# Chunked attention with a spectral mixing layer on one core: the whole hand-written order of steps exchanged for another

## The chip, the core and the metric

One core of one Trainium2 chip runs the kernel. The metric is device time in microseconds (us) of one execution. Five engines work in parallel, each through its own instructions strictly in the order written: TensorE (PE, with its weight loads PEld), VectorE (DVE), ScalarE (ACT), GpSimd (POOL, which here issues all loads) and SyncE (SP, which issues most of the stores). Semaphores hold an instruction back until what it reads is written and what it overwrites has been read.

## What is computed

```python
q_c, k_c, v_c = (t.reshape(B, H, nc, 64, D) for t in (q, k, v))   # B=8, H=8, S=576=9*64, D=64
scores = scale * q_c @ k_c.transpose(...)           # 64 x 64 in each chunk
attn = softmax(scores)
x = (attn @ v_c)  -> [B, S, 512]
theta = x @ w_theta
zr, zi = x * cos(theta), x * sin(theta)
y = w_tok_r @ zr + w_tok_i @ zi                     # mixes the 576 tokens of a batch entry
u = x + y
out = u + max(u @ w_ch, 0)
```

Inputs are fp32 in DRAM; the loads turn them into fp16.

## The kernel before

The eight batch entries are worked in four pairs, 0 to 3. The 1,152 tokens of a pair are cut into five groups: A and B (256 tokens each of the pair's first entry), C and D (256 each of its second), and M, the 64 tokens left over from each entry together (128). All work is cut into small steps, and the string `ORDER` at the top of the file lists them, 584 in all. A loop at the end runs over that string and emits the instructions of each step; the order of the string is therefore the order of each engine's instructions, and the scheduler changes nothing in it. A step reads `kind.pair-group.bank`: `F.1C.2.4` is step F for group C of pair 1 in PSUM banks 2 and 4. A digit behind the kind (`V0`, `H1`) is half of the group's step: half of the heads, or one of two token tiles. There are eight PSUM banks of 128x512 fp32, shared by name: a step that writes a bank waits until the last reader of that bank is done.

The steps, in the order in which a group goes through them:

| step | engine | what it does, and where |
|---|---|---|
| qF, kF, q, k | POOL | loads of q and k of a group (`load_qk`); one DMA each, 256 KB as written; for M two each |
| v | POOL | load of v of a group (`load_v`), three DMAs of 128, 64 and 64 KB; for M two |
| lt, lc, lw | POOL | loads of w_theta, w_ch, and the two token matrices |
| F, FL, N, L, T | PE | transposes of q and k (`qk_t`): F is 64 transposes of 64x64, line 301; FL 32 of 128x64, line 316; for M, N 8 of 128x128 (line 335), L 16 of 128x64, T 32 of 64x64 (line 352) |
| tq, tqA, tk.. | DVE, ACT | their copies out of PSUM; A or V names the engine (`qk_copy`) |
| S, e | PE, ACT | scores (line 405); exp (line 422) |
| V, n | PE, DVE | attention times v (line 440); division by the row sums (lines 452 and 454) |
| X, Q and xA, xV | PE, then ACT or DVE | transpose of x, 8 of 128x128 (X, line 478) or 32 of 64x64 (Q, line 487), and its copy |
| H, g, z | PE, ACT, DVE | x times w_theta (line 518); cos and sin (lines 532, 536); the products zr and zi |
| TW, twA, twV, jw | PE, ACT, DVE | transposes of the token matrices, their copies and sums |
| YA to YM, y | PE, DVE | token mixing of pair 0, one group of inputs at a time; addition to x |
| ja to jd, Ka to Km, ra to rh | DVE, PE, DVE | token mixing of the other pairs by seven block products over sums of z (Ka .. Km: line 693), and their additions |
| U, R and uA, uV | PE, then ACT or DVE | as X and Q, of u |
| W, w, s, sA | PE, DVE, SP or ACT | u times w_ch (line 518), relu and addition, store |
| D | PE | dummy matmuls on zeros; their results are not used |
| pe, pg | ACT | a tiny exp or sin, ahead of the real ones, so that ACT loads the table of that function early; without one the first real exp or sin after the other function loads it |

Loads of pairs 1 to 3 are held back: ahead of each stands a tiny POOL copy (`gate`, line 170) that reads the result of the last n step emitted so far. All loads go through one queue on POOL and land mostly in the order in which they were issued.

The core of the loop:

```python
    with tc.manual_schedule():
        for step in ORDER:
            kind, at, *bank = step.split(".")
```

Of the kernel before, what the change touches and what calls it, by code (L numbers as in the profile page):

```python
# [23 lines left out]
V1.0B.6 kF.1D kF.1A qF.2A xV0.0A kF.2A v.1C V1.0M.1 n1.0B H0.0A.0 g0.0A qF.1B kF.1B H1.0A.3 q.1M
k.1M n1.0M v.1D X0.0B.1 n0.0M TW.03.4 X.0M.2 lc.00 xV0.0B H0.0B.1 z.0C X1.0B.0 TW.02.6 v.1A
xV.0M H.0M.2 twA.03 TW.01.4 z0.0A twA.02 z.0D g.0M xV1.0B TW.00.6 twV.01 twV.00 jw.00 g0.0B
H1.0B.0 qF.2B g1.0B z.0M F.1C.2.4 tqA.1C tkA.1C YC.0C.6 z1.0B YD.0C.6 z0.0B YM.0C.6 S.1C.4 g1.0A
FL.1A.0 FL.1D.2 e.1C y.0C FL.2A.6 YB.0A.4 tkA.1D tqA.1D z1.0A v.2A tq.1A tkA.1A YM.0A.4 S.1D.2
e.1D YA.0A.4 y.0A YB.0B.0 V0.1C.2 qF.2D tqA.2A tkA.2A F.1B.4.5 n0.1C tq.1B V1.1D.6 YA.0B.0
U.0A.2 n1.1D tkA.1B V0.1D.6 S.1B.4 e.1B uV.0A YM.0B.0 W.0A.2 n0.1D V1.1C.4 y.0B S.1A.6 e.1A  # L30
lw.04 X.1D.0 N.1M.1 xA.1D tkA.1M v.1M n1.1C YM.0D.4 w.0A kF.2D YD.0D.4 V0.1A.2 S.2A.6 tq.1M
S.1M.0 e.1M n0.1A v.2C jw.01 YC.0D.4 y.0D e.2A Q.1C.0 xA.1C V1.1A.6 n1.1A H.1D.2 V1.2A.0 V0.2A.4
H.1C.6 n1.2A V1.1M.0 n0.2A pg.00 g.1D V0.1M.1 Q.1A.4 qF.2C U.0D.2 n0.1M X.2A.3 v.1B xV.1A uV.0D
g.1C TW.04.1 n1.1M xA.2A H.1A.4 twA.04 X.1M.0 H.2A.6 kF.2B Y.0M.1 F.2D.2.3 v.3D z.1D v.2M g.1A
g.2A V1.1B.4 tqA.2D z.1C jc.1D z.1A Ka.1A.6 xA.1M y.0M n1.1B ja.1C v.2D tkA.2D F.2B.0.1 qF.3D
V0.1B.4 H.1M.2 tqA.2B n0.1B q.2M g.1M ra.1A q.3M U.0B.3 uA.0B X.1B.0 xV.1B W.0D.4 jb.1D H.1B.2
kF.3D z.1M Kf.1C.6 k.2M tkA.2B Ke.1C.0 g.1B kF.2C w.0D rc.1C S.2D.2 pe.00 e.2D z.1B R.0C.4 v.2B
Kg.1D.6 uV.0C re.1D W.0C.2 N.2M.4 rg.1B w.0C tkV.2M Km.1D.6 rf.1D tqA.2M Kc.1D.0 sA.0A S.2B.2
e.2B V1.2D.6 rd.1C FL.2C.4 qF.3A V0.2D.0 tkA.2C n1.2D n0.2D Kb.1B.2 qF.3B X.2D.0 U.0M.1 v.3B
z.2A rb.1A uV.0M W.0B.6 kF.3A s.0D tqA.2C qF.3C S.2C.4 S.2M.2 s.0C w.0B s.0B xA.2D W.0M.0 w.0M  # L40
e.2C V0.2B.6 n0.2B V1.2C.4 n1.2C v.3C U.1D.1 e.2M uV.1D H.2D.2 V0.2M.0 V1.2M.4 V0.2C.6 n0.2C
n0.2M v.3M Y.1M.5 pg.00 g.2D Q.2C.6 xA.2C V1.2B.0 jd.1B kF.3B W.1D.2 n1.2B y.1M H.2C.0 g.2C z.2D
w.1D s.1D X.2B.5 xA.2B n1.2M Kd.1B.6 z.2C R.1A.0 s.0M F.3A.2.3 uA.1A tqA.3A rh.1B H.2B.4 tkA.3A
X.2M.0 ja.2C jb.2D Ka.2A.6 W.1A.2 xA.2M g.2B ra.2A H.2M.0 F.3D.1.4 w.1A R.1C.2 g.2M uA.1C jc.2D
tqA.3D k.3M z.2M Kf.2C.6 Ke.2C.2 W.1C.0 tkA.3D rc.2C Kg.2D.6 re.2D w.1C S.3D.0 S.3A.4 Kc.2D.2
pe.00 e.3D z.2B e.3A rg.2B rd.2C kF.3C Km.2D.6 v.3A V1.3A.0 n1.3A F.3C.5.4 tqA.3C rf.2D Y.2M.3
tkA.3C S.3C.0 V0.3A.4 FL.3B.6 y.2M e.3C tqA.3B n0.3A V0.3C.0 T.3M.2 tkA.3B n0.3C tkV.3M U.1M.4
tqA.3M uV.1M X.3A.5 Kb.2B.0 xV.3A jd.2B R.1B.2 uV.1B s.1A rb.2A V1.3C.6 n1.3C H.3A.4 pg.00 g.3A
V0.3D.2 W.1B.0 R.2C.6 Q.3C.4 uA.2C n0.3D Kd.2B.2 w.1B S.3M.0 xV.3C pe.00 e.3M s.1B S.3B.4 e.3B
rh.2B H.3C.6 V1.3D.0 z.3A pg.00 g.3C n1.3D V1.3B.2 W.2C.4 n1.3B s.1C w.2C X.3D.0 W.1M.1 w.1M  # L50
R.2D.6 R.2B.4 V1.3M.3 xA.3D n1.3M uA.2D V0.3M.2 H.3D.0 uA.2B n0.3M z.3C g.3D Q.3M.6 V0.3B.4
xA.3M W.2D.2 n0.3B ja.3C Q.3B.4 xA.3B z.3D w.2D R.2A.0 jb.3D Ka.3A.6 uA.2A H.3M.5 jc.3D g.3M
W.2A.0 s.2C H.3B.2 g.3B w.2A ra.3A z.3M Ke.3C.4 re.3D W.2B.0 Kf.3C.6 w.2B s.2B sA.1M rc.3C
Kc.3D.4 z.3B Kg.3D.6 jd.3B sA.2D Kb.3B.0 rg.3B Km.3D.6 rd.3C Y.3M.2 rb.3A R.3A.0 y.3M sA.2A
rf.3D Kd.3B.4 uA.3A R.3D.6 R.3C.0 uA.3C rh.3B uA.3D W.3A.2 w.3A sA.3A W.3C.0 w.3C R.3B.6 uV.3B
s.3C R.3M.2 uA.3M W.3D.4 w.3D sA.3D W.3B.0 w.3B s.3B U.2M.7 uA.2M W.3M.2 w.3M s.3M W.2M.7 w.2M
sA.2M
""".split()


# [794 lines left out]
```

## Time and profile before

| | us |
|---|---|
| median of 3 runs | 205.39 (205.13 to 206.38) |
| the profiled execution | 204.54 |
| its span (first to last recorded event) | 202.8 |
| busy: PE / DVE / ACT / POOL | 190.6 / 148.3 / 120.8 / 83.2 |
| dummy matmuls (line 280) among PE's | 11.8, 39 matmuls |
| ACT table loads | 10 of 1.28 each |

Busy times are sums over the span of one profiled execution; matmuls overlap in the pipeline, so that a matmul's own 0.38 us stands for 0.22 us of progress in a row of them. The execution profiled is 0.85 us below the median of the runs.

### The profile page before, as it was taken

Reading aid. Unit: us, or ns where it says so; the run is one execution under the profiler, and the core shown is the slowest. Engines: PE = TensorE matmul, PEld = TensorE weight load, DVE = VectorE, ACT = ScalarE, POOL = GpSimd, SP = SyncE. Lnnn points to the kernel's source line nnn. Section 1 sums busy time; section 2 is a strip of 40 time slices with the busy share of each in tenths; the row PEclk is TensorE's granted clock in tenths of the full one; section 3 lists DMA queues with packets and bytes.
Section 4 is the critical chain, followed back from the end, with each engine's and each line's share of the span. In section 5 each row is a group of like instructions: output and inputs, shape, how many; then the busy total and the mean of one; then the engine's idle time right before and its main releaser. Section 6 shows DMA issues by size and latency. Waiting matters only on the chain.

```text
span 202.8 us, 7586 instructions
## 1 busy us (share of the span) xinstructions
PE 190.6 (94%) x3409; PEld 102.4 (51%) x3409; DVE 148.3 (73%) x235; ACT 120.8 (60%) x147; POOL 83.2 (41%) x135
## 2 busy tenths in 40 slices
PE   7696889999999999999999999999999999999990
PEld 3353555657556465545655554546544554444540
DVE  0123557984386888898988996978787999896671
ACT  2181498898545898973458296935869884101410
POOL 7967958556965478993084480000000000000000
PEclk9997999999999999999999999999999999999999
DMA  5999999999999969999989999300005200720176
GB/s 63 194 167 169 143 177 202 196 188 171 141 169 149 85 68 134 98 149 210 273 92 184 171 195 105 108 3 3 3 3 210 103 3 5 257 105 0 43 270 207
DMA packets 70431, 26.44 MB, mean 130 GB/s; under 512 B 47232, under 2 KB 65792, under 8 KB 70400
## 3 DMA queue, kind: packets, MB, share of 16 engines
q0 software_dynamic: 65408, 16.54, 87.1%
q1 hardware_dynamic: 3312, 6.29, 8.8%
q10 hardware_dynamic: 1680, 3.15, 4.4%
q8 instruction: 26, 0.43, 0.9%
q14 instruction: 5, 0.04, 0.1%
HBM read 33.06 MB, written 9.44 MB: 210 GB/s over the span
## 4 chain that ended last, share of the span: by engine, by line
PE 86%; POOL 4%; DMA 4%; DVE 2%; issue 1%; ACT 1%; DVEq 0%; POOLq 0%
PE ps L518 32%; PE ps L693 21%; PE ps L604 8%; PE ps L590 4%; DMA v<-in_v_dram 4%; PE ps L478 4%; PE ps L440 3%; PE ps L487 3%; PE ps L316 3%; PE ps L405 3%; POOL qk L181 2%; POOL v L232 2%; PE ps L301 2%; PE ps L269 2%; PE ps L280 1%
## 5 line engine op out<-in xcount | busy, mean ns | idle before, releaser
L232 POOL DMA_DIRECT2D v<-in_v_dram x48 | 36.1, 770 | 3.4 <-issue 1.5
L518 PE MATMUL ps<-wtheta,xT 128*128 128x512 f16 x144 | 34.7, 380 | 0.0
L518 PE MATMUL ps<-wch,uT 128*128 128x512 f16 x144 | 34.0, 380 | 0.0
L712 DVE TENSOR_TENSOR x<-ps,x 128x1024 f16<-128x1024 f32 x24 | 29.1, 1220 | 5.2 <-PE ps L693 4.9
L532 ACT ACTIVATE cos<-ps,pihalf 128x1024 f16<-128x1024 f32 (+1 forms) x22 | 21.1, 959 | 13.9 <-PE ps L518 11.5
L733 DVE SCALAR_TENSOR_TENSOR o<-ps,x 128x1024 f32<-128x1024 f32 (+1 forms) x20 | 22.2, 1116 | 6.5 <-PE ps L518 6.1
L454 DVE TENSOR_TENSOR x<-ps,recip 128x512 f16<-128x512 f32 (+1 forms) x40 | 25.5, 638 | 1.4
L422 ACT ACTIVATE eT<-ps 128x1024 f16<-128x1024 f32 (+1 forms) x18 | 16.5, 929 | 14.1 <-PE ps L405 14.0
L501 ACT COPY uT<-ps 128x1024 f16<-128x1024 f16 (+1 forms) x12 | 11.1, 943 | 20.0 <-PE ps L487 16.8
L372 ACT COPY kT<-ps 128x1024 f16<-128x1024 f16 (+1 forms) x18 | 16.6, 927 | 10.3 <-PE ps L301 5.4
L518 PEld LDWEIGHTS <-uT 128*128 128x128 f16 x144 | 13.2, 98 | 14.8 <-ACT uT L501 0.4
L518 PEld LDWEIGHTS <-xT 128*128 128x128 f16 x144 | 12.8, 98 | 13.9 <-issue 0.3
L370 ACT COPY qT<-ps 128x1024 f16<-128x1024 f16 (+2 forms) x15 | 12.9, 859 | 10.7 <-DVE kT L368 4.4
L536 ACT ACTIVATE sin<-ps 128x1024 f16<-128x1024 f32 (+1 forms) x22 | 19.0, 864 | 0.0
L693 PE MATMUL ps<-z,wT 128*128 128x512 f16 x72 | 18.8, 379 | 0.1
L452 DVE RECIPROCAL recip<-ps 128x8 f32<-128x8 f32 (+1 forms) x40 | 7.9, 196 | 14.3 <-PE ps L440 14.3
L604 PE MATMUL ps<-z,wT 128*128 128x512 f16 x72 | 16.7, 380 | 0.2 <-issue 0.2
L693 PE MATMUL ps<-zsum,wsum 128*128 128x512 f16 x72 | 16.7, 379 | 0.0
L693 PEld LDWEIGHTS <-wsum 128*128 128x128 f16 x96 | 9.1, 98 | 10.8
L280 PE MATMUL ps<-zeros 128*128 128x512 f16 x39 | 11.8, 457 | 2.9 <-issue 1.7
L693 PEld LDWEIGHTS <-wT 128*128 128x128 f16 x96 | 8.8, 98 | 9.8 <-issue 0.5
L723 DVE TENSOR_TENSOR x<-ps,x 128x1024 f16<-128x1024 f32 (+1 forms) x8 | 7.6, 954 | 7.7 <-PE ps L604 5.9
(68 smaller groups left out, 284.8 us busy)
## 6 DMA issues: line engine op xcount, KB each, us to landing
out_dram<-o SPq DMA_DIRECT2D x11, 512.0 KB, 3.5
qk<-in_q_dram POOLq DMA_DIRECT2D x16, 256.0 KB, 7.3
qk<-in_k_dram POOLq DMA_DIRECT2D x16, 256.0 KB, 6.9
v<-in_v_dram POOLq DMA_DIRECT2D x40, 64.0 KB, 5.1
out_dram<-o ACTq DMA_DIRECT2D x5, 512.0 KB, 3.2
v<-in_v_dram POOLq DMA_DIRECT2D x16, 128.0 KB, 6.1
wnat<-in_moe_w_tok_r_dram POOLq DMA_DIRECT2D x2, 288.0 KB, 7.5
wnat<-in_moe_w_tok_i_dram POOLq DMA_DIRECT2D x2, 288.0 KB, 7.9
```

Source lines behind the costliest of these rows:

```text
L232: nc.gpsimd.dma_start(v16[rows, slot + tile, :, 0:D], v[2 * p + bb, :, t0 : t0 + m, :].rearrange("h s d -> s h d"),)
L280: nc.tensor.matmul(psum(bank, 1), zeros[:, 0:P], zeros)
L372: nc.scalar.copy(out=t.rearrange("p x s c -> p x (s c)").rearrange("p x (c s) -> p x c s", s=n), in_=ps.rearrange("p x s c -> p x c s"),)
L422: nc.scalar.activation(out=eT.rearrange("p h r e c -> p (h r e) c"), in_=ps, func=AF.Exp, scale=scale)
L454: nc.vector.tensor_tensor(out=tokens(p, g, "x")[:, :, f * NE * D : (f + 1) * NE * D].rearrange("p c (h d) -> p c h d", h=NE), in0=psv[:, 0 ...
L518: nc.tensor.matmul(ps[:, a * DM : a * DM + cols.stop - cols.start], xT[:, b0 + a, db, :], weight[:, db, cols], start=(db == 0), stop=(db = ...
L532: nc.scalar.activation(out=cos[:, 0:n].rearrange("p a e -> p (a e)"), in_=pin, func=AF.Sin, bias=pihalf, scale=1.0,)
L536: nc.scalar.activation(out=sin[:, 0:n].rearrange("p a e -> p (a e)"), in_=pin, func=AF.Sin)
L604: nc.tensor.matmul(ps[:, a * DM : a * DM + DM], wT[:, kt, t0 : t0 + P], zs[bb], start=(done + k == 0), stop=(done + k == NK - 1),)
L693: nc.tensor.matmul(ps[:, a * DM : a * DM + DM], wt, zt, start=fresh and i == 0, stop=i == len(terms) - 1, skip_group_check=to in ("x", "z"),)
L712: nc.vector.tensor_tensor(out=u, in0=st[p]["ps_k", frm], in1=u, op=ALU.add)
L733: nc.vector.scalar_tensor_tensor(out=o, in0=ps[:, 0 : n * m].rearrange("p (j d) -> p j d", j=n), scalar=0.0, in1=u, op0=ALU.max, op1=ALU.add,)
```

## The change

Only the string `ORDER` is another; the functions that it calls are the same. It has 581 steps. Both orders begin with pair 0. Up to the first token mixing they read (before with -, after with +):

```diff
-qF.0C init.00 kF.0C D.12.0 id.00 D.6.0 F.0C.0.1 tkA.0C qF.0D kF.0D tq.0C S.0C.0 FL.0D.2 tkA.0D
-qF.0A kF.0A v.0C e.0C tq.0D D.8.6 S.0D.6 FL1.0A.0 FL0.0A.2 tq0.0A e.0D tqA1.0A v.0D D.6.4
-V0.0D.4 n0.0D qF.0B tkA0.0A S0.0A.2 tkA1.0A V1.0D.6 n1.0D e0.0A kF.0B D.7.0 FL0.0B.0 tqA0.0B
-tkA0.0B FL1.0B.6 V0.0C.4 q.0M n0.0C V1.0C.2 n1.0C k.0M N1.0M.0 N0.0M.1 tq0.0M tqA1.0M tkA1.0B
-S0.0B.4 X.0C.2 tq1.0B tkV0.0M e0.0B S1.0A.6 e1.0A v.0A lt.00 v.0B S1.0B.4 X.0D.3 xV.0C tkV1.0M
-S1.0M.6 V1.0A.0 xV.0D v.0M e1.0B e1.0M V0.0A.4 n1.0A S0.0M.2 e0.0M H.0C.6 n0.0A pg.00 g.0C
-X1.0A.0 lw.02 lw.00 X0.0A.1 qF.1C V0.0B.2 n0.0B kF.1C H.0D.4 xA1.0A V0.0M.2 g.0D qF.1A qF.1D
...
+qF.0A kF.0A id.00 init.00 D.12.0 qF.0D D.5.0 FL1.0A.0 kF.0D FL0.0A.2 tqA1.0A tq0.0A tkA1.0A
+S1.0A.0 tkA0.0A F.0D.7.6 tq.0D tkA.0D D.5.2 S.0D.2 e1.0A S0.0A.4 e0.0A v.0A qF.0C D.2.0 V0.0A.0
+qF.0B V1.0A.4 n0.0A kF.0B D.6.0 FL0.0B.0 e.0D FL1.0B.2 kF.0C F.0C.6.7 tkA0.0B tqA0.0B n1.0A
+X1.0A.4 tkA.0C tq1.0B v.0D X0.0A.5 D.3.0 V0.0D.0 tq.0C q.0M k.0M n0.0D lt.00 xV0.0A tkA1.0B
+S1.0B.2 V1.0D.6 n1.0D e1.0B S.0C.0 L0.0M.2 L1.0M.3 e.0C tkV0.0M tkV1.0M X.0D.5 xV.0D tq1.0M
+tqA0.0M S0.0B.0 e0.0B S0.0M.6 S1.0M.0 e1.0M H.0D.2 xV1.0A e0.0M v.0C V0.0C.0 V1.0C.4 pg.00 g.0D
+n0.0C n1.0C H1.0A.7 H0.0A.6 v.0B V1.0B.0 n1.0B v.0M lw.02 Q.0C.4 xA.0C g1.0A V0.0M.2 n0.0M g0.0A
+V0.0B.0 V1.0M.3 H.0C.4 lw.00 qF.1C kF.1C n0.0B X0.0B.0 n1.0M qF.1A kF.1A X1.0B.1 z.0D xV1.0B
+Q.0M.2 xA.0M qF.1B kF.1B v.1C TW.02.6 twV.02 H.0M.3 g.0C TW.03.1 twA.03 q.1M k.1M xV0.0B z1.0A
+z.0C H1.0B.0 v.1A g.0M z0.0A qF.2A v.1D TW.01.6 twV.01 H0.0B.1 g0.0B z.0M TW.00.4 F.1C.3.2 tq.1C
+twA.00 jw.00 YD.0D.6 g1.0B z1.0B YC.0D.6 F.1A.0.1 tkA.1C S.1C.2 pe.00 e.1C YM.0C.4 tq.1A YM.0D.6
...
+V0.1B.6 YM.0B.2 n0.1B z.1C YB.0B.2 e.1D y.0B FL.2A.0 qF.2B tqA.2A V1.1D.6 q.2M V0.1D.4 n0.1D
...
+z.1M v.3D e.2D tqA.2B kF.3D Kg.1D.2 rg.1B X.2A.0 xV.2A Ke.1C.4 re.1D tkA.2B v.2M Km.1D.2 qF.3B
...
```

The pair-0 loads before come as q and k of C, D and A, then v of C and D, q and k of B and M, v of A, w_theta, v of B and M, token matrices. After they come as q and k of A and D, v of A, q and k of C and B (q.C, q.B, k.B, k.C), v of D, q and k of M, w_theta, v of C, B and M, token matrices. The steps that are counted otherwise over the whole string:

| step | before | after |
|---|---|---|
| dummy matmuls in the D steps | 39 | 33 |
| full q, k transposes as FL / F, halves counted as halves | 8 / 8 | 3 / 13 |
| M's q, k transposes as N / L / T, two halves as one | 3 / 0 / 1 | 2 / 2 / 0 |
| X / Q of groups A to D, two halves as one; of M | 11 / 5; 3 / 1 | 10 / 6; 1 / 3 |
| U / R of groups A to D; of M | 4 / 12; 3 / 1 | 6 / 10; 2 / 2 |
| copies of q, k, x, u and the token matrices on ACT / DVE, steps | 61 / 32 | 58 / 35 |
| pg / pe steps | 5 / 3 | 7 / 3 |
| changes of ACT's table between exp and sin, by the order of e and g | 9 | 13 |

More of the change, by code (lines that the diff above doesn't have):

```diff
@@ L23 @@
-X1.0A.0 lw.02 lw.00 X0.0A.1 qF.1C V0.0B.2 n0.0B kF.1C H.0D.4 xA1.0A V0.0M.2 g.0D qF.1A qF.1D
[L24 to L57, printed above, removed]
+qF.0A kF.0A id.00 init.00 D.12.0 qF.0D D.5.0 FL1.0A.0 kF.0D FL0.0A.2 tqA1.0A tq0.0A tkA1.0A
+S1.0A.0 tkA0.0A F.0D.7.6 tq.0D tkA.0D D.5.2 S.0D.2 e1.0A S0.0A.4 e0.0A v.0A qF.0C D.2.0 V0.0A.0
@@ new lines @@
+Q.0M.2 xA.0M qF.1B kF.1B v.1C TW.02.6 twV.02 H.0M.3 g.0C TW.03.1 twA.03 q.1M k.1M xV0.0B z1.0A
+z.0C H1.0B.0 v.1A g.0M z0.0A qF.2A v.1D TW.01.6 twV.01 H0.0B.1 g0.0B z.0M TW.00.4 F.1C.3.2 tq.1C
+twA.00 jw.00 YD.0D.6 g1.0B z1.0B YC.0D.6 F.1A.0.1 tkA.1C S.1C.2 pe.00 e.1C YM.0C.4 tq.1A YM.0D.6
+y.0D YC.0C.4 tkA.1A z0.0B F.1B.0.1 qF.1D kF.1D V0.1C.2 v.1B S.1A.6 lw.04 tq.1B YD.0C.4 e.1A y.0C
+n0.1C kF.2A lc.00 tkA.1B YA.0A.6 V1.1A.0 n1.1A V0.1A.4 YB.0A.6 v.1M V1.1C.0 n0.1A S.1B.2 L.1M.4
+qF.2C e.1B X.1A.5 qF.2D xA.1A n1.1C X.1C.0 kF.2C YM.0A.6 U.0D.1 H.1A.2 xV.1C pg.00 g.1A tq.1M
@@ new lines @@
+uV.0D H.1C.0 tkV.1M kF.2D F.1D.5.4 tkA.1D y.0A jw.01 v.2A R.0C.6 g.1C tq.1D uV.0C YA.0B.2 S.1D.4
+V0.1B.6 YM.0B.2 n0.1B z.1C YB.0B.2 e.1D y.0B FL.2A.0 qF.2B tqA.2A V1.1D.6 q.2M V0.1D.4 n0.1D
+W.0D.2 S.1M.4 k.2M n1.1D w.0D X.1D.6 kF.2B TW.04.7 tkA.2A e.1M v.2D twV.04 V1.1M.0 V0.1M.1
+S.2A.2 xA.1D e.2A V1.1B.4 n1.1B n0.1M z.1A H.1D.6 n1.1M X.1B.5 pg.00 g.1D xV.1B W.0C.2 w.0C
+ja.1C R.0A.0 X.1M.4 uA.0A sA.0C z.1D qF.3A jc.1D U.0B.5 H.1B.6 uA.0B v.2C g.1B xA.1M W.0A.0
+Ka.1A.2 w.0A F.2C.4.5 F.2D.0.1 ra.1A tq.2D tkA.2C tkA.2D sA.0D jb.1D qF.3D Y.0M.7 V0.2A.0 n0.2A
@@ new lines @@
+z.1B tqA.2C H.1M.6 y.0M N.2M.4 tkA.2M g.1M Kf.1C.2 S.2D.0 tqA.2M F.2B.7.6 V1.2A.4 rc.1C n1.2A
+z.1M v.3D e.2D tqA.2B kF.3D Kg.1D.2 rg.1B X.2A.0 xV.2A Ke.1C.4 re.1D tkA.2B v.2M Km.1D.2 qF.3B
+U.0M.1 rf.1D H.2A.6 pg.00 g.2A uV.0M Kc.1D.4 jd.1B S.2C.0 pe.00 e.2C q.3M v.2B s.0A rd.1C
+V0.2D.6 n0.2D Y.1M.2 S.2B.6 kF.3A y.1M V0.2C.0 n0.2C e.2B k.3M Kb.1B.4 z.2A V1.2C.6 qF.3C kF.3C
+S.2M.0 e.2M n1.2C W.0B.2 rb.1A V1.2D.0 n1.2D Q.2C.6 W.0M.4 U.1C.5 w.0B s.0B v.3A w.0M U.1A.0
+uV.1C X.2D.1 xA.2C H.2C.2 xV.2D V1.2M.4 V0.2B.6 uA.1A V0.2M.5 pg.00 g.2C n1.2M n0.2B H.2D.0
@@ new lines @@
+W.1A.6 g.2D n0.2M Q.2M.4 xA.2M F.3A.2.3 F.3D.0.1 z.2C w.1A V1.2B.4 n1.2B tkA.3D W.1C.6 tqA.3A
+ja.2C z.2D X.2B.1 w.1C H.2M.2 xA.2B Kd.1B.4 tkA.3A tqA.3D g.2M H.2B.6 rh.1B v.3C s.0M S.3A.0
+jb.2D kF.3B R.1D.2 Ka.2A.4 g.2B v.3B Ke.2C.6 z.2M uA.1D ra.2A Kf.2C.4 F.3C.2.3 e.3A V0.3A.0
+jc.2D tkA.3C re.2D n0.3A tqA.3C rc.2C Kc.2D.6 rd.2C V1.3A.0 n1.3A S.3D.2 e.3D Kg.2D.4 z.2B rg.2B
+S.3C.6 s.1A e.3C Q.3A.0 W.1D.2 U.1B.6 v.3M Km.2D.4 xA.3A H.3A.0 w.1D rf.2D V0.3C.2 n0.3C R.1M.4
+uV.1M uA.1B W.1B.6 sA.1C jd.2B F.3B.2.3 N.3M.4 pg.00 g.3A z.3A w.1B Kb.2B.0 tqA.3B tkA.3B
@@ new lines @@
+V1.3C.2 tqA.3M rb.2A S.3B.6 pe.00 e.3B Y.2M.5 n1.3C tkV.3M Q.3C.0 xA.3C V0.3D.6 y.2M n0.3D
+S.3M.2 W.1M.4 e.3M w.1M U.2C.5 uA.2C V1.3D.0 V1.3M.2 n1.3D s.1B V0.3M.3 n0.3M n1.3M H.3C.6 pg.00
+g.3C V0.3B.0 sA.1M Q.3D.4 xV.3D Kd.2B.2 n0.3B rh.2B V1.3B.0 n1.3B R.2D.6 uA.2D W.2C.4 w.2C
+Q.3B.0 xV.3B R.2B.6 z.3C uA.2B H.3D.2 g.3D R.2A.0 ja.3C uA.2A Q.3M.6 xA.3M z.3D jb.3D H.3B.4
+Ka.3A.2 ra.3A H.3M.0 g.3M z.3M Ke.3C.6 Kf.3C.2 sA.2C re.3D rc.3C W.2A.0 g.3B z.3B w.2A Kc.3D.6
+rd.3C W.2D.4 w.2D jc.3D Kb.3B.0 W.2B.4 jd.3B Kg.3D.2 rb.3A Kd.3B.0 rg.3B Km.3D.2 w.2B R.3A.6
@@ L58 @@
+rh.3B s.2B Y.3M.4 rf.3D s.2A y.3M uA.3A sA.2D R.3C.0 R.3D.2 R.3B.6 W.3A.4 uA.3C w.3A W.3C.0 w.3C
+uA.3B sA.1D U.3M.4 uA.3D W.3D.2 s.3A w.3D W.3B.0 sA.3C R.2M.2 sA.3D uV.3M w.3B s.3B W.3M.4 w.3M
+s.3M uA.2M W.2M.7 w.2M sA.2M
 """.split()
```

## Prediction

> **What bounds the kernel now.** I read the page first, then windows of 5 us over the start, then the chain that ended last in order of time.
>
> ```profile
> span 202.8 us, 7586 instructions
> PE 190.6 (94%) x3409; PEld 102.4 (51%) x3409; DVE 148.3 (73%) x235; ACT 120.8 (60%) x147; POOL 83.2 (41%) x135
> ...
> PEclk9997999999999999999999999999999999999999
> ...
> PE 86%; POOL 4%; DMA 4%; DVE 2%; issue 1%; ACT 1%; DVEq 0%; POOLq 0%
> ```
>
> PE is busy 94% of the span and carries 86% of the chain; the granted clock dips once, in the fourth slice.
>
> ```profile
> core 0: us, PE busy (x) PEld busy (x) DVE busy (x) ACT busy (x) POOL busy (x), PEclk, DMA share, GB/s
> 10.00:15.00 5.00, 5.00 (x103) 3.01 (x98) 1.12 (x2) 3.87 (x5) 3.16 (x5) 1.00 2.08 167
> 15.00:20.00 5.00, 3.06 (x54) 1.51 (x54) 1.70 (x4) 1.20 (x3) 3.65 (x6) 0.75 1.90 171
> 20.00:25.00 5.00, 4.14 (x100) 2.86 (x98) 2.27 (x7) 2.44 (x5) 4.93 (x7) 0.91 1.43 142
> 25.00:30.00 5.00, 4.17 (x106) 2.66 (x104) 3.31 (x8) 4.20 (x8) 3.09 (x6) 1.00 1.83 173
> 30.00:35.00 5.00, 5.00 (x76) 2.74 (x77) 3.27 (x10) 4.10 (x7) 3.80 (x7) 1.00 1.27 203
> ```
>
> Up to 30 us PE has holes while the loads run at full rate; from 30 us on it has none. The chain says the same:
>
> ```profile
> 9.81 7.84 DMA v<-in_v_dram
> ...
> 18.50 2.83 PE ps L280 x7
> ...
> 30.20 0.25 PE ps L440 x16
> 30.45 1.83 PE ps L518 x8
> ...
> 45.80 2.80 PE ps L316 x96
> ...
> 197.70 0.04 DVEq L733
> ```
>
> The first v rows hold the chain until 17.65, dummies (line 280) take 2.83 more, and from 30.45 (step H.0D) to 197.70 it is almost only PE. Where it passes through DVE (137.2, 142.6) the timeline shows PE on other steps meanwhile. So the kernel is a start of 30 us, bound by loads, and 167.2 us of PE work. I price the two by themselves: what PE has left to do, and how much is done when the loads let go.
>
> **PE's work as a whole.** Progress per step, from the chain: F 0.64; FL 0.97 (three in 2.80, single ones 1.03 and 1.01); S 0.38 (M 0.26); a half of V 0.25 (M 0.13); X 0.45 and Q 0.38 (M 0.22 and 0.19); H or W 1.78 (1.73 or 1.83); N 0.45; TW 0.62. Five FL become F: 5 x (0.97 - 0.64) = 1.65 less. M's transposes: L has no row; 16 transposes of 128x64 at FL's 0.03 are 0.48 against N's 0.45, between zero (N's price) and 0.2 for both. I take 0.03 each, and one T (32 in the 0.38 of Q's like) becomes N or L: together 0.13 more. X, Q, U, R exchange plain and small ones: one plain more, one small fewer in the groups (+0.07), three M's the other way (-0.09): nothing. All matrix products are as many as before. Sum: **1.5 less**.
>
> **The start.** In both orders the loads ahead of the token matrices are the same set, and v of M is the last of them. So its landing carries over:
>
> ```profile
> 23.05 1.40 POOL L222 DMA_DIRECT2D v<-in_v_dram  x2
> ...
> v<-in_v_dram POOLq DMA_DIRECT2D x2, 64.0 KB, 6.6
> ```
>
> Issued at 23.05 and 23.75, with a median of 6.6 us to land: 29.7 to 30.3; I take 30.2. In the new order V0.0M, which needs it, cannot start earlier. Done by then, before (at 30.38): one F, three FL, S of all groups, N, V of C, D, A and half of B, X of C, D, A, H of C: 0.64 + 2.91 + 1.78 + 0.45 + 1.75 + 1.35 + 1.78 = 10.7. After, ahead of V0.0M: two F, two FL, the same S, L, the same V, X of A and D, Q of C, H of D and A: 1.28 + 1.94 + 1.78 + 0.48 + 1.75 + 0.90 + 0.38 + 3.56 = 12.1. That is **1.4 more done** at nearly the same time (0.2 earlier).
>
> Can it be done by 30.2? Loads land by their place in the queue, 256 KB of q or k in some 1.35 us: q and k of A at 5.5 and 6.9, of D by 9.6, where C and D landed before. v of A follows at 11 to 12, ahead of its exp (the A copies, D's two copies, one and a half exps run on ACT from 7.5 to 12.7), so the 7.84 us that the chain spent on v are not waited out. k of B and C land at 15 to 17.4, v of D at 19 to 20, M at 21.9 as before, w_theta at about 24 (two v groups come later than it). H.0D then runs from 24.1 to 26, v of C lands at 26 to 26.5, V.0C and H.0A end at 28.8, v of B lands at 28.5 to 29.4, Q.0C ends at 30.0. There is 1.4 of slack between 24.1 and 30.2 in 4.7 of work. The H that follows V0.0M needs xA.0C, an ACT copy of 1.0 from 30.0 to 31.0, while the three V steps end at 30.7: a wait of **0.35**. Of the six dummies fewer none is on the path where loads are waited for.
>
> **Behind the start.** ACT is the tight engine from 30 to 42: xA.0C, g1.0A, g0.0A, xA.0M, g.0C, twA.03, g.0M, g0.0B, twA.00, g1.0B come to 1.0 + 0.6 + 2.1 + 2 x 1.1 + 5 x 1.3 = 12.4, then tkA.1C 1.0, a table load and exp 2.5, tkA.1A 1.0: 46.9, when PE comes to F.1B, which needs that bank. It just fits. The first pair-1 load is gated on n0.0M (about 31) instead of n0.0A (28.2), and stands behind the same 5.0 MB, which landed at 37.0, k of C at 38.3; F.1C comes to PE at 38.8. Both covers have only 0 to 0.5 us of room; if they are gone it costs what they are late. Then the table loads:
>
> ```profile
> 44.92 1.28 ACT L422 ACT_TABLE_LOAD   x1
> 46.22 1.02 ACT L422 ACTIVATE eT<-ps 128x1024 f16<-128x1024 f32 x1
> ```
>
> They rise from 9 changes to 13, 4 x 1.48 (with the tiny activation of 0.20) = 5.9 of ACT, which loses three copies (3.0) to DVE (3 x 0.69). Behind S.2D stand F.2B, V1.2A and Kg.1D, 0.64 + 0.25 + 1.75 = 2.64 of PE; then X.2A wants the bank that e.2D reads, behind tqA.2M 0.6, table 1.28 and exp 1.02 = 2.9: **0.3** late. At e.1D 3.4 of PE stand against 2.3, at e.3A 6.3 against 5.5: hidden, with about 1 to spare. The tail keeps its form: W.3M, W.2M, the last add and store.
>
> **Sum.** -1.5 - 1.4 - 0.2 + 0.35 + 0.3 = -2.45. The profiled execution, 204.54, would be 202.1; the median of 205.39, which is 0.85 above it, **202.9**. By itself this forecast reaches from 201.2 (no new wait, FL at 1.03) to 204.2 (1.3 more in waits at the two tight covers). Chance 0.62.
>
> **Rivals.**
>
> *The start gives nothing* (0.11). The holes move behind v of C and B, whose landings spread (v took 1.4 to 3.6 us a group in the queue), and only the 1.5 of transposes remains: 203.9. For it: the same bytes ahead of V0.0M. Against: they leave 1.4 of slack.
>
> *The clock drops at a worse place* (0.07). The granted clock in windows of 1 us, before:
>
> ```profile
> 17.00:18.00 1.00, 0.72 (x30) 0.46 (x32) 0.00 (x0) 0.00 (x0) 1.00 (x2) 0.76 1.77 179
> 18.00:19.00 1.00, 1.00 (x42) 0.65 (x31) 0.84 (x3) 0.60 (x1) 1.00 (x2) 0.50 2.32 154
> 19.00:20.00 1.00, 1.00 (x4) 0.30 (x2) 0.86 (x3) 0.00 (x0) 0.70 (x2) 0.50 2.09 147
> 20.00:21.00 1.00, 1.00 (x4) 0.30 (x2) 0.00 (x0) 0.00 (x0) 0.93 (x2) 0.53 2.15 132
> ```
>
> Half speed for 3.4 us in all, after PE had idled 1.66 from 15.0; 47% busy from 7 to 10 had not done it. The new order has short holes of 0.3 to 0.8 all through 13 to 24, 6 dummies fewer, and the work from 24.1 to 30.2 where the drop would hurt. One stretch of 3.4 there loses 1.7 less the slack of 1.4, two lose 3.4 less 1.4 = 2.0: 203.2 to 204.9. [...]
>
> *ACT takes over through its table loads* (0.20), the slower case. If all four added loads land on the path, 5.9 on top: 208.8. It decides against the old time from 2.45 of the 5.9 on, and is slower by over 1% (207.44) from 4.5 on. For it: three of the four have no pe step ahead, so they stand between scores and exp; ACT is contiguous from 30 to 42; DVE, which takes three copies, has stretches in the last 25 us with 10 of work for 10 of PE. Against: ACT is busy 60%, it waited 14.0 us on scores and 11.5 on H at the exps and cosines, and each of the three pairs above has PE work in between.
>
> **Chances.** A measurement of this kernel tells about 1% from no change: 203.3 to 207.4. The forecast lies near its lower end: 0.44 of its 0.62 below, 0.18 within; the first two rivals (0.18) within; the third 0.20 above. Faster 0.44, same 0.36, slower 0.20. Range: 201.2 to 207.6, up to where the third rival begins to be slower.
>
> **What would show it.** Right: V0.0M near 30.2 with 12 us of PE work done; PE without holes from 31; line 316 (FL) at 96 instructions for 256; 14 table loads with PE busy beside them. Wrong: idle time of PE ahead of line 440 or 478 with ACT's exp as releaser (third rival); a clock of 0.5 in 24 to 31 (second); V0.0M or H.0C well behind 31 (first); or F.1C waiting for k of pair 1.

## The result, and the profile after

The changed order takes **204.51 us** (median of 20 executions, 202.21 to 207.04) against 205.31 for the old one (20 executions, 204.43 to 206.70) in the same session. The ratio is **0.9919, interval 0.9895 to 0.9944**, which is 1.7 us faster (1.1 to 2.2). The ratio leaves out executions that were disturbed, which the two medians contain, and so it is lower than their quotient. (The two counts of steps above stand the wrong way round: the old string has 581 steps, the new one 584.)

| us | before | after |
|---|---|---|
| the profiled execution | 204.54 | 205.10 |
| its span | 202.8 | 203.3 |
| busy PE | 190.6 | 186.4 |
| span less busy PE | 12.2 | 16.9 |
| fastest of 20 executions | 204.43 | 202.21 |

The profiled execution of after is one of its slower ones. PE is busy 4.2 us less, and the span is no shorter. Its page:

```profile
span 203.3 us, 7900 instructions
...
PE 186.4 (92%) x3567; PEld 99.6 (49%) x3567; DVE 150.3 (74%) x238; ACT 124.4 (61%) x150; POOL 83.3 (41%) x134
...
PEclk9999999999999999999999999999999999999999
...
PE 84%; DMA 4%; POOL 3%; issue 3%; ACT 2%; DVE 1%; ACTq 0%; POOLq 0%
```

The dip in the granted clock is gone (0.50 for 3.41 us from 17.52 in before, 1.00 while PE works here), PE has 158 matmuls and as many weight loads more, and "issue" has grown from 1% to 3% of the chain: time in which PE waited for nothing that the profile shows. The windows of 5 us show where:

```profile
core 0: us, PE busy (x) PEld busy (x) DVE busy (x) ACT busy (x) POOL busy (x), PEclk, DMA share, GB/s
15.00:20.00 5.00, 3.69 (x113) 2.57 (x110) 1.53 (x3) 1.81 (x3) 2.49 (x4) 1.00 2.05 154
20.00:25.00 5.00, 3.03 (x130) 2.24 (x128) 3.46 (x10) 3.15 (x6) 5.00 (x8) 1.00 1.43 148
25.00:30.00 5.00, 4.32 (x56) 2.02 (x56) 1.97 (x6) 4.12 (x7) 3.33 (x5) 1.00 1.92 146
30.00:35.00 5.00, 3.93 (x114) 2.48 (x114) 4.22 (x12) 3.16 (x5) 3.17 (x7) 1.00 1.17 190
70.00:75.00 5.00, 3.79 (x107) 2.33 (x106) 3.32 (x6) 3.00 (x5) 3.36 (x7) 1.00 1.83 141
```

From 30 to 35, where before was 5.00 busy, there are holes again, and there is one at 70 to 75. The timeline of PE in after (start, duration, what, and in brackets the idle time ahead of it and its releaser):

```profile
21.95 0.28 PE L405 MATMUL ps<-qT,kT 64*64 64x64 f16 x11 [0.88 <-issue]
...
27.93 0.42 PE L440 MATMUL ps<-v,eT 64*64 64x65 f16 x28 [0.55 <-issue]
...
31.47 0.44 PE L440 MATMUL ps<-v,eT 64*64 64x65 f16 x24 [0.65 <-DVE x L454]
...
34.40 0.38 PE L478 MATMUL ps<-id,x 128*128 128x128 f16 x4 [0.43 <-issue]
...
58.84 0.55 PE L478 MATMUL ps<-id,x 128*128 128x128 f16 x7 [0.81 <-issue]
...
72.60 0.39 PE L518 MATMUL ps<-wch,uT 128*128 128x512 f16 x1 [1.21 <-issue]
```

Five stops without a releaser, 3.88 us in all, and each lies inside a step or between the two halves of one: the last one between the seventh and the eighth matmul of one W, which wait for the same tiles. The chain of waits takes it over whole:

```profile
69.78 1.62 PE ps L518 x7
71.39 1.21 issue
72.60 0.39 PE ps L518
```

Before has such stops as well, in its own timeline of PE:

```profile
16.66 0.59 PE L280 MATMUL ps<-zeros 128*128 128x512 f16 x2 [1.66 <-issue]
...
29.91 0.28 PE L478 MATMUL ps<-id,x 128*128 128x128 f16 x2 [0.70 <-issue]
...
51.43 3.61 PE L604 MATMUL ps<-z,wT 128*128 128x512 f16 x16 [0.19 <-issue]
```

**What these stops are.** I numbered PE's records in the trace (weight loads, matmuls and semaphore instructions, from zero, in order of start). Every stop of 0.19 us or more in both kernels that has no releaser stands ahead of a number 192 + 256n. The trace has a DMA queue of its own that fits: after, then before, in the queue table of each page:

```profile
q8 instruction: 28, 0.46, 0.9%
```

```profile
q8 instruction: 26, 0.43, 0.9%
```

Each packet of this queue is 16 KB (16,384 bytes), and there is about one for every 256 of PE's instructions (28 for 7,149 after, 26 for 6,838 before); that makes 64 bytes for each, an estimate. Their times against the stops, worked out from the packet records of the trace:

| kernel | number | its packet moved | PE went on | stop |
|---|---|---|---|---|
| before | 448 | 13.87 to 15.06 | 16.66 | 1.66 |
| before | 960 | 27.19 to 28.40 | 29.91 | 0.70 |
| before | 1728 | 48.81 to 49.88 | 51.43 | 0.19 |
| after | 704 | 18.75 to 20.30 | 21.95 | 0.88 |
| after | 960 | 25.40 to 26.52 | 27.93 | 0.55 |
| after | 1216 | 31.95 to 32.90 | 34.40 | 0.43 |
| after | 2240 | 56.36 to 57.32 | 58.84 | 0.81 |
| after | 2752 | 69.80 to 70.69 | 72.60 | 1.21 |

PE goes on 1.4 to 1.9 us after the packet has landed. The same holds in the runs below: all 14 profiles together have 54 stops of 0.15 us or more without a releaser, all of them at a number 192 + 256n (give or take two records), and 53 end 1.2 to 1.9 us after the packet for that block landed. In after the packet for 2752 began to move 4.3 us after the block ahead of it was begun (65.54); later, at 111.85, 138.00 and 145.35, a packet began 0.1 to 0.2 us after. The packets of the loads keep the DMA engines busy at 90% or more in that stretch (the queue table of after for 68 to 71 us; the last column adds up the times of all packets, as a share of the 16 engines' time):

```profile
q0 software_dynamic: 2310, 0.51, 188.3%
q8 instruction: 1, 0.02, 1.9%
```

So while the loads run PE gets its instructions at some 256 per 6 to 7 us (the limits 704 to 2752 of after were passed 6.0 to 7.1 us apart, one 4.6), and a stretch with many small matmuls uses them faster: F is 128 instructions (64 matmuls with a weight load each), FL 64. That is my second theory; the experiments are to tell it from the first.

### The profile page after: what moved, and what is told of

Same layout as the page of the kernel before. It is cut to its first block, busy times and chain, and to the rows that moved or that the text cites. A ratio compares the mean times of both kernels' runs of the same rounds, so it can differ in the third digit from the quotient of the medians.

```text
span 203.3 us, 7900 instructions
## 1 busy us (share of the span) xinstructions
PE 186.4 (92%) x3567; PEld 99.6 (49%) x3567; DVE 150.3 (74%) x238; ACT 124.4 (61%) x150; POOL 83.3 (41%) x134
## 4 chain that ended last, share of the span: by engine, by line
PE 84%; DMA 4%; POOL 3%; issue 3%; ACT 2%; DVE 1%; ACTq 0%; POOLq 0%
PE ps L518 32%; PE ps L693 21%; PE ps L604 8%; DMA qk<-in_k_dram 4%; PE ps L590 4%; PE ps L478 4%; PE ps L440 3%; PE ps L301 3%; PE ps L487 3%; PE ps L405 3%; POOL qk L181 2%; PE ps L269 2%; POOL v L232 1%; ACT kT L372 1%; PE ps L316 1%
## 5 line engine op out<-in xcount | busy, mean ns | idle before, releaser
L501 ACT COPY uT<-ps 128x1024 f16<-128x1024 f16 (+1 forms) x14 | 13.6, 982 | 25.8 <-PE ps L487 18.7
L422 ACT ACTIVATE eT<-ps 128x1024 f16<-128x1024 f32 (+1 forms) x18 | 16.5, 926 | 11.5 <-PE ps L405 11.2
L170 POOL COPY seen<-recip 1x1 f32<-1x1 f32 x16 | 3.2, 199 | 37.4 <-DVE recip L452 37.4
L604 PE MATMUL ps<-z,wT 128*128 128x512 f16 x72 | 16.9, 380 | 0.1
L368 DVE COPY qT<-ps 128x1024 f16<-128x1024 f16 (+2 forms) x11 | 6.4, 581 | 14.3 <-PE ps L316 9.3
L370 ACT COPY qT<-ps 128x1024 f16<-128x1024 f16 (+2 forms) x12 | 9.9, 823 | 6.5 <-PE ps L316 5.8
```

The costliest lines, as they stand in the source:

```text
L422: nc.scalar.activation(out=eT.rearrange("p h r e c -> p (h r e) c"), in_=ps, func=AF.Exp, scale=scale)
L501: (nc.vector.tensor_copy if how == "V" else nc.scalar.copy)(out=to.rearrange("p b (r c) -> p b r c", c=CH), in_=psv)
L604: nc.tensor.matmul(ps[:, a * DM : a * DM + DM], wT[:, kt, t0 : t0 + P], zs[bb], start=(done + k == 0), stop=(done + k == NK - 1),)
```

## The experiments

**T1**, the picture of the prediction: PE's work and its waits for data make the time, F is 0.33 us cheaper than FL wherever it stands, and the stops "issue" are chance. **T2**: PE's instructions come in blocks of 256 behind the loads; up to some 75 us what counts is how many instructions PE has to issue and where the limits of the blocks fall. Ratios are to the old kernel in the same session. The twelve kernels ran in three sessions of four, in the order in which they stand here.

**Five transposes back to FL, in after.**

```diff
-F.0D.7.6   F.1A.0.1   F.1D.5.4   F.2C.4.5   F.3B.2.3
+FL.0D.6    FL.1A.0    FL.1D.4    FL.2C.4    FL.3B.2
```

> The new order with the five q, k transposes that it had turned from FL into F (groups 0D, 1A, 1D, 2C, 3B) as FL again: 5 x 32 matmuls fewer, 320 PE instructions fewer with their weight loads, 5 x 0.33 = 1.65 us more of PE progress by the chain. Theory 1 (PE's work sets the end): 1.65 us longer than the new order, ratio to the kernel before about 1.000. Theory 2 (from 20 to 73 us PE waits at every 256th of its instructions until the next 16 KB have come over the instruction queue, so that fewer instructions shorten the stops): at most 0.6 us longer than the new order, ratio 0.991 to 0.995, and the stops ahead of lines 405, 440, 478 and 518 in that stretch (3.9 us in the profile of the new order) shrink by about as much as the transposes grow.

Measured: 208.85 us, ratio 1.0182 (1.0136 to 1.0229). Both theories missed: it is 4 to 5 us slower than after, not 1.65 or less. Its timeline of PE has the limits at other places, and one stop (ahead of 2752) is longer than any in after, but all its stops together are 3.6 us against 3.9, so they do not explain the loss:

```profile
78.58 0.23 PE L440 MATMUL ps<-v,eT 64*64 64x65 f16 x5 [2.85 <-issue]
```

What else its profile has and the first profile of after has not: half the granted clock for 3.4 us from 11.1 and again from 79.3, just behind this stop (an estimate of what that can cost: at most half of it, 3.4 us), and 1.8 us more of waits for loads. How the loss divides between these and the price of five FL is not shown.

**The same five as F, in before.**

```diff
-FL.0D.2    FL.1A.0    FL.1D.2    FL.2C.4    FL.3B.6
+F.0D.2.3   F.1A.0.1   F.1D.2.3   F.2C.4.5   F.3B.6.7
```

> The order before with the same five FL as F. Theory 1: 1.65 us faster than the kernel before, ratio 0.992. Theory 2: 320 PE instructions more, one and a quarter blocks of 256, so part of it is given back in stops without a releaser between 20 and 75 us: 0.3 to 1.0 us faster, ratio 0.995 to 0.9985.

Measured: 216.21 us, ratio 1.0473 (1.0403 to 1.0544), both theories missed by far: the edit that I had priced at 1.65 us of gain costs 10 us. The timeline of PE:

```profile
16.34 1.70 PE L316 MATMUL ps<-id,qk 128*64 128x128 f16 x27 [2.74 <-issue]
...
30.10 0.28 PE L440 MATMUL ps<-v,eT 64*64 64x65 f16 x10 [1.20 <-issue]
...
52.92 0.48 PE L301 MATMUL ps<-id,qk 64*64 64x64 f16 x20 [3.65 <-issue]
```

They stand ahead of 448, 960 and 1728, the three numbers at which before stops for 1.66, 0.70 and 0.19. Of the 9.1 us between the profiled executions (213.68 and 204.54) 7.3 are stops, 9.9 against 2.5 in all; the granted clock is at half for 10.2 us against 3.4, which can add up to 3.4 (an estimate: half of the 6.8 more). The sign is T2's, the size neither had: I had taken the stops as they were and not asked what happens when a limit moves into a stretch of small matmuls.

**Each start with the other's remainder.** The order of after up to F.1C with before's steps behind it, and the reverse.

> The new order up to the last transposes of the token matrices for pair 0 (just ahead of F.1C), then everything that is left in the sequence of the order before. Theory 1 (the start is worth its 1.25 us, with one FL as F 0.33): about 1.5 us faster than before, ratio 0.9925. Rival (the start gives nothing, all of the gain is in the rest): ratio 0.998 to 1.000, and PE comes to F.1C no sooner than before (40.8 us). Theory 2: between, since the start carries 192 PE instructions more up to F.1C and the stops move behind it.

> The order before up to F.1C, then everything that is left in the sequence of the new order. Theory 1: the rest is worth four FL as F, 1.3, less 0.3 for X.2A behind the exp of S.2D: 1.0 us faster than before, ratio 0.995. Rival (the start gives nothing): ratio 0.992, all of the gain. Theory 2: 0 to 0.7 us faster, ratio 0.9965 to 1.000, with stops ahead of lines 478 and 518 near 58 and 72 us as in the new order.

Measured: 221.5 us (ratio 1.0721, 1.0661 to 1.0781) and 213.13 us (1.0368, 1.0325 to 1.0410). Neither tells anything of the question, since the seam makes waits that neither kernel has. The profiled execution of the first, moreover, took 254.56 at a granted clock of 0.745 in the mean, so its waits are only a hint. With after's start q and k of 1A and 1D come too late, with before's start F.1C waits for a bank that a sine holds, and v of pair 1 is late as well; the timelines of PE:

```profile
57.71 3.62 PE L316 MATMUL ps<-id,qk 128*64 128x128 f16 x64 [6.23 <-DMA qk<-in_k_dram]
```

```profile
43.63 1.07 PE L301 MATMUL ps<-id,qk 64*64 64x64 f16 x64 [3.64 <-ACT sin L536]
...
61.86 0.42 PE L440 MATMUL ps<-v,eT 64*64 64x65 f16 x29 [1.78 <-DMA v<-in_v_dram]
```

**After once more, unchanged.**

> The new order unchanged, for a second profile of it and as the measure of the next three. Both theories: 203.7 (0.992 of the kernel before). Theory 2 (PE stops at every 256th of its instructions, at numbers 192 + 256 n, when the next 16 KB of them have not come): stops without a releaser again at those numbers, between 20 and 75 us, but of other lengths, since the loads ahead of each fetch vary.

Measured: 204.04 us (201.79 to 206.31), ratio 0.9844 (0.9780 to 0.9908). The second profile of the same program has its stops ahead of 704, 1984 and 2240: other lengths, and one other place, but all of them 192 + 256n.

```profile
22.99 0.28 PE L405 MATMUL ps<-qT,kT 64*64 64x64 f16 x11 [1.11 <-issue]
...
55.06 1.02 PE L604 MATMUL ps<-z,wT 128*128 128x512 f16 x4 [0.31 <-issue]
...
61.45 0.55 PE L478 MATMUL ps<-id,x 128*128 128x128 f16 x7 [0.60 <-issue]
```

**66 instructions more, PE's time the same.** Eleven of the first dummies, 512 columns wide, become 44 of 128 columns; everything behind them is the same code, a quarter of a block later in the count.

```diff
-id.00 init.00 D.12.0 qF.0D ...
+id.00 init.00 E.44.0 D.1.0 qF.0D ...
+    def narrow(n, bank):
+        for _ in range(n):
+            nc.tensor.matmul(psum(bank, 1)[:, 0:P], zeros[:, 0:P], zeros[:, 0:P])
```

> The new order with eleven of the twelve first dummy matmuls of 512 columns as 44 of 128 columns: the same columns and the same PE time ahead of the first load's landing, 66 PE instructions more, nothing else. Theory 1 (PE's work and the engines' waits set the end): same as the new order within 0.5 us. Theory 2: every later step moves by 66 instructions against the block boundaries, so the stops fall into other steps; the time moves by more than 1 us, up or down, and the stops are again at 192 + 256 n.

Measured: **214.22 us**, ratio 1.0373 (1.0314 to 1.0432), 10 us above after in the same session. T1 has no way to this. The timeline of PE:

```profile
22.55 0.19 PE L305 MATMUL ps<-id,qk 64*64 64x64 f16 x1 [2.60 <-issue]
...
28.66 0.38 PE L409 MATMUL ps<-qT,kT 64*64 64x64 f16 x13 [1.46 <-issue]
...
53.37 0.39 PE L409 MATMUL ps<-qT,kT 64*64 64x64 f16 x25 [2.06 <-issue]
...
58.74 0.35 PE L409 MATMUL ps<-qT,kT 64*64 64x64 f16 x21 [1.42 <-issue]
...
98.58 0.22 PE L444 MATMUL ps<-v,eT 64*64 64x65 f16 x2 [1.35 <-issue]
...
131.86 1.69 PE L522 MATMUL ps<-wch,uT 128*128 128x512 f16 x7 [2.06 <-issue]
```

These stand ahead of 704, 960, 1728, 1984, 3520 and 4800. With three short ones the stops come to 11.8 us, against 3.9 and 2.0 in the two profiles of after. A lower clock is a rival explanation here, and the second profile of after settles it: it has the same dips, half the granted clock for 3.4 us from 11.0 and for 6.8 from 24.6, where this one has 3.4 from 11.5 and 6.8 from 28.6. Between these two profiled executions (206.31 and 216.72) lie 10.4 us, and 9.8 of them are stops. So in these runs the count of instructions sets where PE stops, whatever the work (all 54 stops of the 14 profiles at 192 + 256n): of T2 this much is shown.

**No late v loads.** Pairs 2 and 3 load no v.

```diff
+        if p > 1:
+            return
```

> The new order without the v loads of pairs 2 and 3, which leaves their outputs with v of pairs 0 and 1: 2.4 MB of small packets fewer, issued from about 45 us on; PE, ACT and DVE have the same instructions. Theory 1: nothing, since these loads have 18 us and more of room: within 0.5 us of the new order. Theory 2: the fetches between 45 and 75 us wait less behind loads, the stops there (2.0 us in the first profile) go to under 0.5: 1.5 us faster, up to 2.0.

Measured: 203.46 us, ratio 0.9852 (0.9800 to 0.9903): no different from after. The stop ahead of 2752 is gone, as T2 wants, but after's second profile has none there either; and the ones ahead of 704, 1216, 1472, 1728, 1984 and 2240 (0.91, 0.15, 0.55, 0.44, 1.14, 0.33 us) are there, 3.5 in all. T2's forecast failed: fewer load packets from 45 us on did not end the stops.

**The first v behind q and k of four groups.**

```diff
-S0.0A.4 e0.0A v.0A qF.0C D.2.0 V0.0A.0 qF.0B V1.0A.4 n0.0A kF.0B D.6.0 ...
+S0.0A.4 e0.0A qF.0C qF.0B kF.0B kF.0C v.0A D.2.0 V0.0A.0 V1.0A.4 n0.0A D.6.0 ...
```

> The new order with the first v (of A) behind all of q and k of A, D, C and B, instead of behind A and D. If the early v is what the start gains by: V0.0A, which stands ahead of FL.0B and F.0C on PE, waits until 18 to 19 us instead of 13, and all of the 1.2 us of the start is lost: 1.2 us slower than the new order. If the last first-pair landings (v of B and M at about 30) set the start's end: the wait is taken up before them, 0 to 0.5 us slower.

Measured: 208.98 us, ratio 1.0100 (1.0039 to 1.0161), some 5 us above after in the same session; every theory had less. The timeline of PE:

```profile
17.58 0.26 PE L440 MATMUL ps<-v,eT 64*64 64x65 f16 x2 [4.44 <-DMA v<-in_v_dram]
...
35.98 0.22 PE L440 MATMUL ps<-v,eT 64*64 64x65 f16 x4 [0.65 <-DVE x L454]
```

V0.0A waits 4.44 us for its v, and V0.0B, at 31.47 in after, comes 4.5 later, at 35.98. That looks as if the whole wait were carried on, but up to V0.0B PE stands still 9.7 us in all, against 8.8 in after, whose stops ahead of 704 and 960 are missing here. Behind the wait the granted clock is lower (windows, columns as above, with the granted clock third from the end):

```profile
14.00:18.00 4.00, 0.26 (x2) 0.13 (x2) 0.00 (x0) 0.18 (x1) 1.53 (x3) 0.92 2.27 159
18.00:22.00 4.00, 2.74 (x35) 1.38 (x35) 1.71 (x4) 0.00 (x0) 4.00 (x6) 0.50 1.32 93
22.00:26.00 4.00, 4.00 (x109) 2.86 (x107) 1.12 (x2) 1.80 (x3) 3.10 (x5) 0.73 1.66 168
```

It is at half for 6.8 us from 17.4, which can cost up to 3.4 (an estimate), and in all six executions its mean is 0.982 or less. To have v of A behind two groups rather than four is worth about 5 us; two against three was not tried by itself.

**66 instructions more in before.** The same edit of the first dummies.

> The order before with the same 66 PE instructions more ahead of everything as in a_shift66 (eleven dummies of 512 columns as 44 of 128). Theory 1: same as before. Theory 2, worked from the issue times of PE in the profile of before with each block of 256 given 5.6 to 6.2 us up to 70 us and 3.5 behind: stops of 1.5 to 3.8 us in all become 3.0 to 5.4, so about 1.5 us slower (ratio 1.005 to 1.010), far less than the 10 us that the new order lost by it.

Measured: 205.82 us (12 executions), ratio 0.9939 (0.9897 to 0.9981): 0.6% faster, where I had 1.5 us slower. The stop ahead of 448 shrinks from 1.66 to 0.67 and those ahead of 960 and 1728 go; one of 1.32 ahead of 2240 takes their place. But the profiled execution, 206.76, is one of the longest of the 12, and PE waits there 1.3 us more for loads in the first 42 us than in before; so the gain is not shown to be in the stops. T2 is right that the shift moves the stops and was wrong about the sign here; my model of when a packet starts is not good enough to forecast it.

**Four other transposes as FL.** 256 instructions fewer, so that the limits behind 3B lie on the same code as in after.

```diff
-F.2B.7.6   F.3D.0.1   F.3C.2.3   F.3B.2.3
+FL.2B.6    FL.3D.0    FL.3C.2    FL.3B.2
```

> The new order with four transposes behind 85 us (groups 2B, 3D, 3C, 3B) as FL: 4 x 64 = 256 PE instructions fewer, exactly one block, so that the boundaries ahead of 88 us and behind 142 us lie in the same steps as in the new order, and in a stretch where a block of 256 takes 4 to 10 us. Theory 1 (an FL costs 0.33 us of PE more than an F): 1.3 us slower than the new order (a_again, 204.0). Theory 2 says the same here, since no stops stand there; if it is the number of instructions that costs everywhere: no slower, or faster.

Measured: 205.53 us (12 executions), ratio 1.0003 (0.9969 to 1.0038), against 0.9919 for after: 0.84% or 1.7 us more, where four times 0.33 is 1.3 (against the 0.9844 of the other session it would be 3.3). The traces say it more sharply. The last stop of this profile is at 74.45, ahead of all four, and in none of the three profiles is there a stop or a dip of the granted clock behind 85 us until PE is done. From the transposes F.2C to the last W, in after, then here:

```profile
85.23 1.27 PE L301 MATMUL ps<-id,qk 64*64 64x64 f16 x128
...
196.00 1.90 PE L518 MATMUL ps<-wch,uT 128*128 128x512 f16 x8
```

```profile
87.08 1.27 PE L301 MATMUL ps<-id,qk 64*64 64x64 f16 x128
...
199.77 1.90 PE L518 MATMUL ps<-wch,uT 128*128 128x512 f16 x8
```

That is 110.77 us in after (110.76 in its second profile) and 112.69 here. So where PE's blocks are there in time, an F is cheaper than an FL as the prediction had it, but by 0.48 rather than 0.33: 1.92 for the four.

**F.0C as FL, with 64 instructions more ahead of it,** to take the limit 704 out of the small matmuls and leave all behind it in place.

```diff
-... D.12.0 ... F.0C.6.7 ...
+... E.43.0 D.1.0 ... FL.0C.6 ...
```

> The new order with F.0C as FL (64 PE instructions fewer) and 64 more in the first dummies (43 of 128 columns for eleven of 512): from F.0C on (18 us) every step keeps its place against the block boundaries, ahead of it all are 64 later. Theory 1: 0 to 0.33 us slower. Theory 2: the boundary at 704, where PE stopped for 0.9 and 1.1 us in the two profiles of the new order, follows a block that began earlier: 0.5 to 1.2 us faster, with the later stops as in the new order.

Measured: 205.77 us (12 executions), ratio 0.9990 (0.9955 to 1.0024): a miss, 1.4 us slower than after (by its 0.9919). The stop ahead of 704 is gone, but one of 2.32 comes ahead of 448, and the granted clock falls behind it:

```profile
PEclk9995799999999999999999999999999999999999
```

```profile
15.79 0.43 PE L444 MATMUL ps<-v,eT 64*64 64x65 f16 x25 [2.32 <-issue]
```

**F.0D, F.0C and F.1D as FL, with 100 instructions more ahead.**

> The new order with F.0D, F.0C and F.1D as FL (192 PE instructions fewer) and 100 more in the first dummies. Theory 1: 3 x 0.33 = 1.0 us slower at most. Theory 2, worked from the issue times as above: stops fall from 3.7 to 4.4 us to about 1.5, the transposes cost 0.6: 1.5 us faster than the new order, the fastest so far (ratio to the kernel before about 0.98).

Measured: 203.37 us (202.80 to 206.56), ratio 0.9883 (0.9841 to 0.9926). Its profiled execution takes 202.80, with one stop left (0.62 us ahead of 960). It beats the old kernel, but its interval overlaps those of after (0.9895 to 0.9944, and 0.9780 to 0.9908), so it is no shown improvement on it.

## Why the prediction was right, and what was wrong in it

**The direction and about two thirds of the size.** 2.45 us of gain were forecast, 1.7 (1.1 to 2.2) measured. The fastest execution, 202.21, is where the sum had put one like the profiled execution of before (202.1); the profiled one is 3 above it, with 3.88 of stops. That the time came out so near is in part luck: the same order with 66 instructions more takes 214.22, and nothing in the prediction's sum would have moved.

**"Behind the start" left out the supply of instructions**, and this is the step that failed. "From 30 us on it has none" (holes) was read from before and carried over. The change puts 158 more matmuls, each with a weight load, into PE's stream, and the packets with its instructions come among those of the loads (1 beside 2,310 from 68 to 71 us). From F.1C to the end after takes 162.8 us and before 162.0. The step prices of the prediction give after 1.1 less work there; the stops are 0.81 + 1.21 against 0.19, 1.8 more; that leaves 0.1 of the difference (some 0.7 if each F saves the 0.48 found above). In this execution the transposes' gain behind the start was given back as stops. The longest stop at one limit was 3.65 us (five F in before, ahead of 1728).

**PE's work as a whole: the sign of the price was right, its size too small, its place not asked.** Four FL cost 1.92 where 1.3 was priced, at places without stops. With most of the five among the loads, five F in before cost 10 us, 7.3 of the 9.1 between the profiles in stops: there the position of the block limits outweighs the price. That five FL in after cost 4 to 5 is not explained by stops; beside the five prices (2.4 at 0.48 each) stand the lower clock (up to 3.4 by the estimate above) and 1.8 more of waits for loads in that profile, and their shares are not shown.

**The start: V0.0M right, F.1C not.** V0.0M ran at 30.51 (30.2 forecast), with the steps ahead of it that the prediction lists; v of M had landed at 30.06. The 1.66 us at 15.0 and the 0.70 at 29.91 in before were no holes that loads or copies make, as I had them, but waits for instructions: PE went on 1.60 and 1.51 after the packet had landed. After has two such stops ahead of V0.0M, 0.88 and 0.55, and a wait of 0.68 for an exp; H.0D came at 25.32 where I had 24.1, and with that the "1.4 of slack" was nearly used up. Without the stops V0.0M could have run at most 0.45 earlier, since its v was not there. F.1C came at 40.50, 1.7 behind the 38.8 forecast: 0.3 of it at V0.0M, 0.3 since V0.0B waited 0.65 for the normalization n1.0B (DVE, line 454) where I had H wait 0.35 for xA.0C, and 0.43 in the stop ahead of 1216; the other 0.7 is in no wait, the steps between took 8.9 where their prices gave 8.2. From there to F.1B (48.57) it took 8.07 for 8.1 forecast: ACT's tight cover held.

**X.2A 0.3 late** did not come. The wait of that size is at 93.27, 0.25 for an add on DVE (line 712).

**The rivals.** *The start gives nothing* (0.11) fits the profiled execution better than its chance: at F.1C after is 0.2 us ahead (40.50 against 40.73), with 0.4 less work done by the prices. Its cause was not the spread of the landings. *The clock drops* (0.07): not in the first profile, in the second it did. The windows of after's second profile (columns as above) show half speed where the rival had it:

```profile
20.00:24.00 4.00, 2.36 (x93) 1.58 (x92) 2.33 (x6) 2.20 (x5) 3.95 (x6) 1.00 0.97 130
24.00:28.00 4.00, 3.34 (x59) 2.30 (x59) 2.19 (x6) 2.76 (x6) 2.95 (x5) 0.58 2.26 156
28.00:32.00 4.00, 4.00 (x42) 1.59 (x41) 0.99 (x3) 2.64 (x4) 1.81 (x3) 0.57 1.40 150
```

That execution took 206.31. Of the 20 executions of after, the seven with a mean granted clock of 0.986 or less took 205.4 in the median, the others 203.6: some 1.9 us, in about one execution of three, near the 2.0 that the rival gave. With the six of the repeat it is 11 executions of 26, and 7 of 51 for the kernel before in the three later sessions: this rival came true in part, and it takes from the gain. Ahead of this dip PE had stopped for 1.11 and was 2.36 busy of 4.00; ahead of the one in before it had stopped for 1.66, and a stop of 1.21 in the first profile of after was followed by none. What length of idling brings a dip is not shown. (From 7 to 10 us PE was busy 1.31 of 3.00 in before, 44%, not 47%.) *ACT takes over* (0.20) did not happen: 14 table loads as counted, and PE waited for no exp behind 31 us.

**What stays open.** How the 1.7 us divide between cheaper transposes, the start, the clock and a lucky position of the limits: the exchanged halves were spoiled by their seams, and 66 instructions alone gain 0.6% in before and lose 5% in after. And what exactly starts a packet: the forecasts of the single shifts above did not hold.

## What to carry to other kernels

Where PE stops in the middle of a step with no releaser, count its instructions in the trace: here all 54 stops stood at 192 + 256n, and 53 of them ended 1.2 to 1.9 us after a packet of the instruction queue had landed. There many small matmuls beside the loads cost more than their own time: five F for FL in before, priced at 1.65 us of gain, cost 10. Then look at the granted clock of the two profiles before calling the rest a wait: here a stop was several times followed by some microseconds at half the clock (1.11 us by 6.8 from 24.6 in after's second profile, 2.85 by 3.4 from 79.3 with five FL in after). Price an edit that adds or removes instructions there by a shift of nothing but the count, before believing a sum of durations. And compare two orders by many executions of each: here one profile pair had the sign reversed.

## What the runs showed of the hardware that was not expected

- 66 instructions more in the first 6 us, with the first transposes of q and k at 6.89 instead of 6.82, cost 10 us (204.04 to 214.22 us), 9.8 of the 10.4 between the two profiles in stops, some as far away as 131 us.
- At 53 of the 54 stops PE went on 1.2 to 1.9 us after the packet for that block had landed. Among the loads the packet began to move up to 4.3 us after the block ahead was begun in after (5.1 for the first one in before); from 111 us on in after it began at most 0.9 us after that, or before it.
- One program stops at other block limits, and for other lengths, from execution to execution: 3.88 us in the one profile of after, 2.02 in the other.
- While PE worked, the granted clock fell to 0.50 for 3.41 or for 6.83 us at a time, in 12 of the 14 profiles; the profiled execution of after's start with the rest of before had 0.745 in the mean over its 252.5 us.
